# Attention of the first chunks in M2's PSUM banks, v of chunk 1 over ScalarE's queue, M1 begun with one batch, q, k and v prepared one chunk ahead

## Chip, cores, metric

One core of a Trainium2 chip. The metric is the kernel's device time in microseconds (us). The hardware profiler records one execution; its span, from the first to the last instruction, is about 1.8 us shorter than the time of the same run (234.0 against 235.79). Engines: PE is TensorE, DVE VectorE, ACT ScalarE, POOL GpSimd, SP SyncE; ACTq, SPq and POOLq are the profile's lines for ScalarE, SyncE and GpSimd issuing a DMA. The granted clock is the share of full speed that the profile shows for TensorE. A completion semaphore is what a DMA counts up in the built program and a later instruction waits on; the profile puts such a wait down to the DMA's landing (2.17 us for iden in the run before). An eviction is the kernel's copy of a result from a PSUM tile to an SBUF tile (0.59 us on ScalarE and 0.69 on VectorE for 128x512).

## The reference

```python
def _attn_ref(q, k, v):                       # q, k, v: (4 batches, 8 heads, 768, 64)
    gamma = 1.0 - 2.0 ** (-5.0 - np.arange(H, dtype=np.float32))
    for t in range(S):                        # retention: a decayed state per head
        state = gamma[None, :, None, None] * state + np.einsum('bhd,bhe->bhde', k[:, :, t], v[:, :, t])
        y[:, :, t] = scale * np.einsum('bhd,bhde->bhe', q[:, :, t], state)

def _moe_ref(x, w_in, w_out):                 # x: y with heads side by side, (3072, 512); d_ff 2048
    h = x @ w_in
    g = 0.5 * h * (1.0 + np.tanh(c * (h + 0.044715 * h * h * h)))
    return g @ w_out
```

## The kernel before

The 768 positions are worked in 6 chunks of 128. For each chunk and batch, attention is T (transposes of q and k), A (scores, masked on eviction) and Y (y, and the new state S). Then come M1 (h = x w_in by 16 feature blocks of 128 columns, "fc", followed by gelu on ScalarE) and M2 (g w_out). The kernel divides its PSUM banks into tags: att 3, h 3, o 2. Below, v(1,0) means v of chunk 1, batch 0. A unit is one feature block of M1, or a quarter of one batch's M2; a piece is T, A or Y of one batch (T2 is T of batch 2). Units and pieces are dealt in turn, which is meant to keep matmuls running while a piece is evicted. Spin matmuls are fillers without a result.

```python
    def load(c, b):                                   # all of chunk c, batch b over SyncE's queue
        for nm in "qkv":
            load1(nc.sync, nm, c, b)
    def hold(nm, c, b, until):                        # writes one element of a load's buffer:
        nc.gpsimd.tensor_copy(out=ld_tile(nm, c, b)[0:1, 0, 0:1], in_=until)   # the load waits for `until`
    ...
    # --- end of the head ---
    hold("q", 1, 0, w_in_sb[3][0:1, 0, 0:1])
    for b in range(B):
        load(1, b)
    for b in range(B):
        prep(1, b)                                    # q, k scaled, v cast to f16, on GpSimd
        if b == 2:
            for i in range(NO):
                load_w_out(i)                         # GpSimd's queue
    hold("q", 2, 0, w_out_sb[2][0:1, 0, 0:1])
    for b in range(B):
        load(2, b)
    for fc in range(2):
        moe1(0, fc, half, 2 * half)
    for fc in range(2, NF - 1):
        moe1(0, fc)
    ...                                               # attention and M1 of chunk 1
    for b in (0, 2):                                  # M2 of chunk 0: two batches in turn
        for fc in range(NF):
            moe2(0, b, [fc])
            moe2(0, b + 1, [fc])
        ev_O(0, b)
        ev_O(0, b + 1)
    for b in range(B):
        prep(2, b)
    for b in range(B):
        load(3, b)
    zip_units([u for b in range(B) for u in units2(1, b)], pieces(2, STD))
    for c in range(2, NCk):
        if c + 1 < NCk:
            for b in range(B):
                prep(c + 1, b)
        ...
```

## Time and profile before

| | before |
|---|---|
| median of 4 runs | 238.26 us (235.75 to 238.79) |
| profiled run | 235.79 us, span 234.0, granted clock 1.0 |
| TensorE busy | 219.7 us, 94% |
| first M1 at full rate | from 21.95 us |
| M2 of chunk 0 starts | 59.34 us |

Shares of busy time say little here, because the stages have different limits. What a part is worth is read from TensorE's idle stretches, stage by stage. The prediction shows these lines.

### The profile page before, as it was taken

Reading aid. Unit: us, or ns where it says so; the run is one execution under the profiler, and the core shown is the slowest. Engines: PE = TensorE matmul, PEld = TensorE weight load, DVE = VectorE, ACT = ScalarE, POOL = GpSimd, SP = SyncE. Lnnn points to the kernel's source line nnn. Section 1 sums busy time; section 2 is a strip of 40 time slices with the busy share of each in tenths; the row PEclk is TensorE's granted clock in tenths of the full one; section 3 lists DMA queues with packets and bytes.
Section 4 is the critical chain, followed back from the end, with each engine's and each line's share of the span. In section 5 each row is a group of like instructions: output and inputs, shape, how many; then the busy total and the mean of one; then the engine's idle time right before and its main releaser. Section 6 shows DMA issues by size and latency. Waiting matters only on the chain.

```text
span 234.0 us, 3976 instructions
## 1 busy us (share of the span) xinstructions
PE 219.7 (94%) x1623; PEld 117.2 (50%) x1623; DVE 84.2 (36%) x150; ACT 80.3 (34%) x146; POOL 81.1 (35%) x96
## 2 busy tenths in 40 slices
PE   7857998999999999599999999999999999999993
PEld 2435445788534555244544544544554545444453
DVE  3497008760001567424445324444424333200001
ACT  2636661368211111145511155511155511267220
POOL 3584189339650011793101699910000000000000
PEclk9999999999999999999999999999999999999999
DMA  7999999999950988199011199511110011100112
GB/s 177 288 174 181 207 243 199 191 180 237 209 168 39 275 203 249 59 259 254 18 45 45 48 218 233 134 45 45 49 45 0 3 45 45 69 23 0 45 45 90
DMA packets 83537, 29.71 MB, mean 127 GB/s; under 512 B 75584, under 2 KB 80576, under 8 KB 83520
## 3 DMA queue, kind: packets, MB, share of 16 engines
q1 hardware_dynamic: 72528, 23.71, 40.1%
q0 software_dynamic: 4752, 4.19, 12.0%
q10 hardware_dynamic: 6240, 1.57, 3.0%
q8 instruction: 12, 0.20, 0.4%
q14 instruction: 5, 0.04, 0.0%
HBM read 27.37 MB, written 6.29 MB: 144 GB/s over the span
## 4 chain that ended last, share of the span: by engine, by line
PE 83%; DVE 6%; POOL 4%; ACT 3%; issue 2%; DMA 1%; POOLq 0%; DVEq 0%; ACTq 0%
PE h_ps L320 33%; PE o_ps L340 33%; PE qkT_ps L175 4%; PE a_ps L193 3%; PE y_ps L226 3%; PE spin_ps L112 3%; DVE a_sb L206 2%; PE s_ps L238 2%; POOL q L145 2%; POOL k L145 2%; PE y_ps L216 2%; ACT qkT L167 1%; DVE st L257 1%; ACT o_sb L167 1%; DVE xT L169 1%
## 5 line engine op out<-in xcount | busy, mean ns | idle before, releaser
L340 PE MATMUL o_ps<-w_out,g 128*128 128x512 f16 (+1 forms) x400 | 88.8, 371 | 1.0 <-ACT o_sb L167 0.9
L320 PE MATMUL h_ps<-xT,w_in 128*128 128x512 f16 (+1 forms) x456 | 88.6, 346 | 0.2
L329 ACT ACTIVATE g<-h_ps 128x512 f16<-128x512 f32 (+1 forms) x114 | 60.4, 529 | 65.9 <-PE h_ps L320 64.5
L320 PEld LDWEIGHTS <-w_in 128*128 128x128 f16 x456 | 43.0, 98 | 35.3 <-DVE xT L169 0.5
L340 PEld LDWEIGHTS <-g 128*128 128x128 f16 x400 | 37.3, 98 | 39.6 <-issue 1.9
L206 DVE TENSOR_TENSOR a_sb<-a_ps,mask 128x512 f16<-128x512 f32 x48 | 30.9, 686 | 27.3 <-PE a_ps L193 27.3
L167 ACT COPY o_sb<-o_ps 128x512 f32<-128x512 f32 x18 | 10.4, 586 | 70.8 <-PE o_ps L340 66.2
L266 POOL TENSOR_TENSOR stg<-st,cst 128x512 f32<-128x512 f16 x16 | 16.5, 1040 | 49.7 <-DVE st L257 46.4
L169 DVE COPY qkT<-qkT_ps 128x1024 f16<-128x1024 f16 x20 | 13.8, 691 | 35.8 <-PE qkT_ps L175 35.8
L145 POOL TENSOR_TENSOR k<-k,cst 128x512 f16<-128x512 f32 x23 | 24.5, 1063 | 6.2 <-DMA k<-in_k_dram 6.2
L145 POOL TENSOR_TENSOR q<-q,cst 128x512 f16<-128x512 f32 x20 | 20.9, 1044 | 4.9 <-DMA q<-in_q_dram 4.9
L169 DVE CAST xT<-y_ps 128x512 f16<-128x512 f32 x21 | 14.5, 691 | 22.4 <-PE y_ps L226 22.3
L169 DVE COPY o_sb<-o_ps 128x512 f32<-128x512 f32 x5 | 3.5, 692 | 28.7 <-PE o_ps L340 28.7
L257 DVE TENSOR_TENSOR st<-s_ps,stg 64x256 f16<-64x256 f32 x32 | 13.3, 417 | 0.4
L175 PE MATMUL qkT_ps<-iden,q 128*128 128x128 f16 x96 | 9.3, 219 | 3.7 <-DVE a_sb L206 1.9
L142 POOL CAST v<-v 128x512 f16<-128x512 f32 x20 | 12.2, 611 | 1.5 <-DMA v<-in_v_dram 1.4
L193 PE MATMUL a_ps<-qkT 64*128 64x128 f16 x192 | 10.2, 219 | 2.0 <-ACT qkT L167 1.2
L193 PEld LDWEIGHTS <-qkT 64*128 64x128 f16 x192 | 5.6, 94 | 12.1 <-issue 7.6
L112 PE MATMUL spin_ps<-zero 128*128 128x512 f16 x31 | 10.4, 472 | 1.2 <-DVE zero L104 1.2
L175 PEld LDWEIGHTS <-q 128*128 128x128 f16 x96 | 7.1, 98 | 8.7 <-POOL q L145 2.3
L226 PE MATMUL y_ps<-a_sb,v 128*64 128x128 f16 x192 | 10.6, 225 | 0.8 <-DVE a_sb L206 0.7
L175 PE MATMUL qkT_ps<-iden,k 128*128 128x128 f16 x96 | 9.3, 220 | 1.0 <-POOL k L145 1.0
(30 smaller groups left out, 71.8 us busy)
## 6 DMA issues: line engine op xcount, KB each, us to landing
out_dram<-o_sb SPq DMA_DIRECT2D x23, 256.0 KB, 2.0
k<-in_k_dram SPq DMA_DIRECT2D x22, 256.0 KB, 4.2
q<-in_q_dram SPq DMA_DIRECT2D x22, 256.0 KB, 4.0
v<-in_v_dram SPq DMA_DIRECT2D x22, 256.0 KB, 4.4
w_out<-in_moe_w_out_dram POOLq DMA_DIRECT2D x4, 512.0 KB, 10.5
w_in<-in_moe_w_in_dram POOLq DMA_DIRECT2D x3, 512.0 KB, 10.2
q<-in_q_dram ACTq DMA_DIRECT2D x2, 256.0 KB, 3.9
v<-in_v_dram ACTq DMA_DIRECT2D x2, 256.0 KB, 5.0
```

Source lines behind the costliest of these rows:

```text
L112: nc.tensor.matmul(out=ps, lhsT=zero[:, 0:128], rhs=zero, start=True, stop=True)
L145: eng.tensor_tensor(out=t, in0=src, in1=cst[:, col:col + H].unsqueeze(2).broadcast_to([128, H, Dh]), op=ALU.mult,)
L169: eng.tensor_copy(out=out, in_=in_)
L175: nc.tensor.transpose(out=ps[:, i, hp], in_=pair(h16[nm, c, b], hp), identity=iden)
L193: nc.tensor.matmul(out=ps[j][:, hp], lhsT=t[j * 64:(j + 1) * 64, 1, hp], rhs=t[j * 64:(j + 1) * 64, 0, hp], start=True, stop=True,)
L206: nc.vector.tensor_tensor(out=s, in0=ps[j], in1=mask[:, j], op=ALU.mult)
L226: nc.tensor.matmul(out=y_ps[j * 64:(j + 1) * 64, hp], lhsT=vv[:, 2 * hp + j], rhs=a_sb[c, b, j][:, hp], start=(c == 0), stop=True, skip_gr ...
L257: nc.vector.tensor_tensor(out=st[sl, :, b, sl], in0=s_ps[sl, :, sl], in1=stg[sl, :, b, sl], op=ALU.add,)
L266: nc.gpsimd.tensor_tensor(out=stg[:, :, b], in0=st[:, :, b], in1=cst[:, OG:OG + NHP].unsqueeze(2).broadcast_to([128, NHP, 128]), op=ALU.mult,)
L320: nc.tensor.matmul(out=h_ps[:, t0:t1], lhsT=w_in_sb[wi][:, kc, wr * 128:(wr + 1) * 128], rhs=xT[c][:, kc, t0:t1], start=(kc == 0), stop=(k ...
L329: nc.scalar.activation(out=g_sb[c, fc][:, t0:t1], in_=h_ps[:, t0:t1], func=AF.Gelu_apprx_tanh, scale=1.0,)
L340: nc.tensor.matmul(out=ps[:, n0:n1], lhsT=g_sb[c, fc][:, b * C:(b + 1) * C], rhs=w_out_sb[fc // (NF // NO)][:, fc % (NF // NO), n0:n1], st ...
```

## The change

It means to fill TensorE's gaps. In chunks 0 and 1 M2 is not yet running, so its two o banks are free for Y and S, and T and A have the att banks to themselves. M1 of chunk 1 begins as soon as one batch is ready, in units of 128 columns. v of chunk 1 is loaded over ScalarE's queue and cast there, to relieve SyncE and GpSimd. M2 of chunk 0 runs in halves. Chunk c+2 is prepared during the attention of chunk c+1. Outputs of three batches are issued by ScalarE.

```diff
-        y_ps = psum.tile([128, NHP, 128], F32, tag="att", bufs=3, name="y_ps")
+        tag, bufs = ("o", 2) if c < 2 else ("att", 3)
+        y_ps = psum.tile([128, NHP, 128], F32, tag=tag, bufs=bufs, name="y_ps")
 ... (s_ps likewise; spin takes tag "h"; w_in in 4 equal loads; head reordered)
-    hold("q", 1, 0, w_in_sb[3][0:1, 0, 0:1])
+    hold("q", 1, 0, w_in_sb[2][0:1, 0, 0:1])
     for b in range(B):
-        load(1, b)
+        load1(SY, "q", 1, b)
+        load1(SY, "k", 1, b)
     for b in range(B):
-        prep(1, b)
+        prep1(PO, "q", 1, b)
+        prep1(PO, "k", 1, b)
         if b == 2:
             for i in range(NO):
                 load_w_out(i)
     hold("q", 2, 0, w_out_sb[2][0:1, 0, 0:1])
     for b in range(B):
         load(2, b)
+    for fc in range(4, NF):
+        if fc == NF - 1:
+            run1("T0")
+        moe1(0, fc)
+        if fc >= 8 and fc % 2 == 0:
+            load1(AC, "v", 1, (fc - 8) // 2)
+    prep1(AC, "v", 1, 0)
 ... (chunk 1: A0, Y0 T1, M1 of blocks 0 to 9 on batch 0 alone around A1 and Y1, then the rest)
     for b in (0, 2):
-        for fc in range(NF):
-            moe2(0, b, [fc])
-            moe2(0, b + 1, [fc])
-        ev_O(0, b)
-        ev_O(0, b + 1)
+        for f0 in (0, hf):
+            for bb in (b, b + 1):
+                moe2(0, bb, range(f0, f0 + hf))
+                if f0:
+                    ev_O(0, bb)
+        load(3, b)
+        load(3, b + 1)
+        prep(2, b)
+        prep(2, b + 1)
-    zip_units([...units2(1, b)], pieces(2, STD))
+    zip_units([...units2(1, b)], std(2))      # std deals prep of chunk c+1 between the pieces
 ... (ev_O: batches 0 to 2 issue their output from ScalarE's queue)
```

More of the change, by code (lines that the diff above doesn't have):

```diff
@@ L109, in spin @@
     def spin(n):
-        ps = psum.tile([128, 512], F32, tag="o", bufs=2, name="spin_ps")
+        ps = psum.tile([128, 512], F32, tag="h", bufs=3, name="spin_ps")
         for _ in range(n):
@@ L235, in mm_Y @@
         if c + 1 < NCk:
-            s_ps = psum.tile([128, NHP, 128], F32, tag="att", bufs=3, name="s_ps")
+            s_ps = psum.tile([128, NHP, 128], F32, tag=tag, bufs=bufs, name="s_ps")
             for hp in range(NHP):
@@ L285, in att_Y @@
         decay(c, b)
-    w_in_n = (2, 2, 4, 4, 4)
+    w_in_n = (4, 4, 4, 4)
     w_in_at = [sum(w_in_n[:i]) for i in range(len(w_in_n))]
@@ L356, in ev_O @@
         o_sb = op.tile([128, d_model], F32, tag="o", name="o_sb")
-        copy_on(nc.vector if b == B - 1 else nc.scalar, o_sb, ps)
-        nc.sync.dma_start(out=rows, in_=o_sb)
+        if b == B - 1:
+            nc.vector.tensor_copy(out=o_sb, in_=ps)
+            nc.sync.dma_start(out=rows, in_=o_sb)
+        else:
+            nc.scalar.copy(out=o_sb, in_=ps)
+            nc.scalar.dma_start(out=rows, in_=o_sb)
     def moe2_last(c, b):
@@ L374, in moe2_last, with std @@
             nc.sync.dma_start(out=rows[:, m0:m2], in_=o_sb[:, m0:m2])
-    fn = {"T": att_T, "A": att_A, "Y": att_Y}
+    fn = {"T": att_T, "A": att_A, "Y": att_Y, "P": prep}
     def pieces(c, names):
         return [(p[0], c, int(p[1])) for p in names.split()]
-    STD = "T0 T1 A0 T2 A1 Y0 T3 A2 Y1 A3 Y2 Y3"
+    def std(c):
+        todo = pieces(c, "T0 T1 A0 T2 A1 Y0 T3 A2 Y1 A3 Y2 Y3")
+        if c + 1 < NCk:
+            for at, b in ((8, 0), (10, 1), (12, 2), (14, 3)):
+                todo.insert(at, ("P", c + 1, b))
+        return todo
     def zip_units(units, todo, over=None):
@@ L392, in zip_units @@
                 done += 1
-    VE, AC, PO = nc.vector, nc.scalar, nc.gpsimd
+    VE, AC, PO, SY = nc.vector, nc.scalar, nc.gpsimd, nc.sync
     half = 2 * C
@@ L414 @@
     prep1(AC, "v", 0, 1)
+    spin(2)
     mm_Y(0, 0)
     ev_Y(0, 0, AC)
-    spin(2)
     prep1(VE, "q", 0, 2)
     prep1(PO, "k", 0, 2)
-    PO.tensor_copy(out=misc[0:1, 1:2], in_=ld_tile("q", 0, 3)[0:1, 0, 0:1])
-    for i in range(len(w_in_n)):
-        load_w_in(i)
     mm_A(0, 1)
     ev_A(0, 1)
-    ev_S(0, 0)
+    spin(2)
+    PO.tensor_copy(out=misc[0:1, 1:2], in_=ld_tile("q", 0, 3)[0:1, 0, 0:1])
+    load_w_in(0)
+    load_w_in(1)
+    prep1(PO, "k", 0, 3)
+    load_w_in(2)
+    load_w_in(3)
     mm_T(0, 2)
@@ L429 @@
     prep1(AC, "v", 0, 2)
+    prep1(VE, "q", 0, 3)
     mm_Y(0, 1)
     ev_Y(0, 1, AC)
-    spin(2)
-    prep1(VE, "q", 0, 3)
-    prep1(VE, "k", 0, 3)
+    ev_S(0, 0)
+    spin(1)
     mm_A(0, 2)
     ev_A(0, 2)
-    ev_S(0, 1)
+    prep1(AC, "v", 0, 3)
+    spin(3)
     mm_T(0, 3)
-    ev_T(0, 3, AC)
-    spin(2)
+    ev_T(0, 3)
+    mm_Y(0, 2)
+    ev_Y(0, 2, AC)
     mm_A(0, 3)
     ev_A(0, 3)
-    prep1(AC, "v", 0, 3)
-    mm_Y(0, 2)
-    ev_Y(0, 2, AC)
-    ev_S(0, 2)
+    ev_S(0, 1)
+    spin(1)
     moe1(0, 0, 0, half)
+    moe1(0, 1, 0, half)
     mm_Y(0, 3)
     ev_Y(0, 3)
+    ev_S(0, 2)
     ev_S(0, 3)
-    moe1(0, 1, 0, half)
     for b in range(B):
         decay(0, b)
-    hold("q", 1, 0, w_in_sb[3][0:1, 0, 0:1])
+    for fc in range(2, 4):
+        moe1(0, fc, 0, half)
+    for fc in range(4):
+        moe1(0, fc, half, 2 * half)
+    hold("q", 1, 0, w_in_sb[2][0:1, 0, 0:1])
     for b in range(B):
-        load(1, b)
+        load1(SY, "q", 1, b)
+        load1(SY, "k", 1, b)
     for b in range(B):
-        prep(1, b)
+        prep1(PO, "q", 1, b)
+        prep1(PO, "k", 1, b)
         if b == 2:
@@ L466, with run1 @@
         load(2, b)
-    for fc in range(2):
-        moe1(0, fc, half, 2 * half)
-    for fc in range(2, NF - 1):
-        moe1(0, fc)
-    run1 = lambda names: [fn[nm](c, b) for nm, c, b in pieces(1, names)]
-    run1("T0")
-    moe1(0, NF - 1)
-    run1("A0 T1")
-    spin(2)
-    run1("Y0 A1")
-    spin(4)
-    run1("Y1")
-    spin(2)
-    zip_units(
-        [(lambda fc=fc: moe1(1, fc, 0, half)) for fc in range(NF)],
-        pieces(1, "T2 A2 Y2 T3 A3 Y3"),
-    )
+    def run1(names):
+        for nm, c, b in pieces(1, names):
+            fn[nm](c, b)
+    for fc in range(4, NF):
+        if fc == NF - 1:
+            run1("T0")
+        moe1(0, fc)
+        if fc >= 8 and fc % 2 == 0:
+            load1(AC, "v", 1, (fc - 8) // 2)
+    prep1(AC, "v", 1, 0)
+    run1("A0")
+    spin(3)
+    run1("Y0 T1")
+    for fc in range(0, 2):
+        moe1(1, fc, 0, C)
+    prep1(AC, "v", 1, 1)
+    run1("A1")
+    for fc in range(2, 7):
+        moe1(1, fc, 0, C)
+    run1("Y1")
+    for fc in range(7, 10):
+        moe1(1, fc, 0, C)
+    prep1(AC, "v", 1, 2)
+    units = [(lambda fc=fc: moe1(1, fc, C, half)) for fc in range(10)]
+    units += [(lambda fc=fc: moe1(1, fc, 0, half)) for fc in range(10, NF)]
+    units.insert(8, lambda: prep1(AC, "v", 1, 3))
+    zip_units(units, pieces(1, "T2 A2 Y2 T3 A3 Y3"))
     for fc in range(NF):
@@ L492, in units2 @@
         return u
+    hf = NF // 2
     for b in (0, 2):
-        for fc in range(NF):
-            moe2(0, b, [fc])
-            moe2(0, b + 1, [fc])
-        ev_O(0, b)
-        ev_O(0, b + 1)
-    for b in range(B):
+        for f0 in (0, hf):
[5 more added lines that the diff above has]
+        load(3, b + 1)
         prep(2, b)
-    for b in range(B):
-        load(3, b)
-    zip_units([u for b in range(B) for u in units2(1, b)], pieces(2, STD))
+        prep(2, b + 1)
+    zip_units([u for b in range(B) for u in units2(1, b)], std(2))
     for c in range(2, NCk):
-        if c + 1 < NCk:
-            for b in range(B):
-                prep(c + 1, b)
         if c + 2 < NCk:
@@ L515 @@
             units += [u for b in range(B) for u in units2(c, b)]
-            zip_units(units, pieces(c + 1, STD), len(units) - 2)
+            zip_units(units, std(c + 1), len(units) - 2)
         else:
```

## The prediction

> **What bounds the kernel now.** I read the busy shares first, then the chain that ended last, then what TensorE waits for, then the timelines of ScalarE, GpSimd and SyncE's queue.
>
> ```profile
> PE 219.7 (94%) x1623; PEld 117.2 (50%) x1623; DVE 84.2 (36%) x150; ACT 80.3 (34%) x146; POOL 81.1 (35%) x96
> ...
> PE 83%; DVE 6%; POOL 4%; ACT 3%; issue 2%; DMA 1%; POOLq 0%; DVEq 0%; ACTq 0%
> ```
>
> TensorE is busy for 94% of 234.0 us and holds 83% of the chain. A change that leaves the arithmetic alone can win only the rest: TensorE's idle stretches and its fillers. Its list of waits says where they lie:
>
> ```profile
> PE qkT_ps L175 <- DVE a_sb L206: 1.9, 2, 1.2
> PE qkT_ps L175 <- POOL q L145: 1.8, 1, 1.8
> ...
> PE a_ps L193 <- ACT qkT L167: 1.2, 2, 0.7
> PE qkT_ps L175 <- POOL k L145: 1.0, 3, 0.6
> PE o_ps L340 <- ACT o_sb L167: 0.9, 2, 0.5
> ```
>
> (Columns: us in total, times, longest.) The POOL rows are the passage from chunk 2 to chunk 3 (a gap of 2.6 us from 96.6 us in TensorE's timeline; the passage to chunk 4 loses only some 0.4). The o_sb row is the second matmul (M2) of chunk 0; the others are the head, before 21.95 us. Fillers (the spin matmuls) cover part of 35.5 to 41.75 us, where chunk 1's attention starts.
>
> Three more places matter for what the change adds. ScalarE's timeline at the start:
>
> ```profile
> 5.41 0.37 ACTq L77 DMA_DIRECT2D q<-in_q_dram  x1
> 6.09 0.47 ACTq L77 DMA_DIRECT2D v<-in_v_dram  x1
> 6.60 0.62 ACT L140 CAST v<-v 128x512 f16<-128x512 f32 x1 [2.17 <-DMA iden<-rr_ident]
> ```
>
> This cast does not read iden. It waited because the v load ahead of it in ScalarE's stream waited for iden's landing: in the built program the hardware-queue DMAs take eight completion semaphores in turn, in the order in which the kernel's text issues them, and a DMA waits on its issuing engine until the DMA eight places earlier, on whatever queue, has landed. GpSimd's timeline (start, length) and SyncE's queue, with the chain that releases chunk 2's loads:
>
> ```profile
> 25.12 0.18 POOL L88 CAST q<-w_in 1x1 f32<-1x1 f16 x1 [1.34 <-DMA w_in<-in_moe_w_in_dram]
> ...
> 37.61 3.05 POOL L309 DMA_DIRECT2D w_out<-in_moe_w_out_dram  x4
> ...
> 50.63 0.18 POOL L88 CAST q<-w_out 1x1 f32<-1x1 f16 x1 [7.37 <-DMA w_out<-in_moe_w_out_dram]
> ...
> 57.61 1.04 POOL L145 TENSOR_TENSOR q<-q,cst 128x512 f16<-128x512 f32 x1 [0.26 <-DMA q<-in_q_dram]
> ...
> 60.53 1.04 POOL L145 TENSOR_TENSOR q<-q,cst 128x512 f16<-128x512 f32 x1 [0.23 <-DMA q<-in_q_dram]
> ...
> 64.35 0.61 POOL L142 CAST v<-v 128x512 f16<-128x512 f32 x1 [1.22 <-DMA v<-in_v_dram]
> ```
>
> ```profile
> 50.84 0.37 SPq L77 DMA_DIRECT2D q<-in_q_dram  x1
> ...
> 54.45 0.82 SPq L77 DMA_DIRECT2D k<-in_k_dram  x1
> ```
>
> Chunk 2's loads are held until the third w_out block has landed (50.63). The one-element cast at L88 is that hold.
>
> [...] the first 14 fillers take 5.58 us (0.40 each), the next three 0.81 (0.27 each).
>
> **The change, part by part.**
>
> *The v loads of chunk 1 on ScalarE's queue.* They stand in ScalarE's stream after the gelus of feature blocks 8, 10, 12 and 14 of chunk 0, but in the text after all loads of chunk 2. Followed through the built program's semaphores: v(1,0) waits for k(2,1), v(1,1) for q(2,2), v(1,2) for v(2,2), v(1,3) for q(2,3). All four stand behind the hold on w_out. So ScalarE, having done gelu 8 at some 29 us, cannot issue v(1,0) until chunk 2's loads have begun to land, and gelu 9 stands behind it. TensorE has three banks for h and stops at some 31 us. It is no deadlock: GpSimd and SyncE do not need ScalarE to get there.
>
> When does it end? The hold on w_in stays at 25.1 us: the tile waited for again completes the first three quarters of w_in. SyncE then issues 8 loads in place of 12, and GpSimd prepares q and k only. Before, q(1,0) was ready to prepare at 28.7. From there three batches of q and k take 6 x 1.02 = 6.1 us, with loads arriving in step, so w_out is issued at 34.9 in place of 37.61. Issue to hold took 50.63 - 37.61 = 13.0 us; with fewer loads in the way I take 12.2: 47.1 us. k(2,1) was issued 54.45 - 50.84 = 3.6 us after the first load, and loads land about 4.1 us after issue (53.60 to 57.61 for q(2,1)): 47.3 + 3.6 + 4.1 = 55.0 us. By the landings 57.61, 60.53, 64.35 and 65.14 of before, less 3.5 us: q(2,2) 57.0, v(2,2) 60.8, q(2,3) 61.6. ScalarE now does: issue v(1,0), gelus 9 and 10 (0.6 each), issue v(1,1) at 57, gelus 11 and 12 to 59, issue v(1,2) at 60.8 to 61.6, gelus 13 and 14 to 62.8, issue v(1,3) to 63.7, gelu 15 to 64.3, cast of v(1,0) to 64.9. Only then may the y matmuls of chunk 1 start: 65.0, where before they stood at 37.2 to 37.6. This is a shift of some 27.5 us.
>
> *From there to M2 of chunk 0.* Before: 37.6 to 59.4, 21.8 us. After, from the rows by stage: M1 of chunk 1 is 64 x 0.216 = 13.8; batches 2 and 3 of attention 2 x (0.45 + 0.33 + 0.89) = 3.3; the rest of batches 0 and 1 2.3: 19.5 us of TensorE's work. Waits remain: about 1.05 us for qkT of batch 1 (DVE does xT 0.69, the state 0.85, qkT 0.69 first), about 1.3 us because units of 128 columns (0.22 us each) are too short to cover evictions, and ScalarE at an estimated 0.33 us for each narrow gelu. That is 21.85 us, no gain. The clock: TensorE comes out of 24 us of idleness with a few matmuls, so I add 1 us for a slow start. Shift at M2: about +28.5.
>
> *M2 of chunk 0 in halves:* the two waits of 0.46 us go: -0.9.
>
> *Preparing one chunk ahead:* the 2.6 and 0.4 us go. But M2 of chunk 1 is 16 units and chunk 2's attention now 16 pieces with the preparations, so its last y lands after the last unit, where before one unit lay behind it. DVE then copies o (0.69) and evicts y (0.69) before M1 may go on: +0.55. Sum -2.5.
>
> *The head.* With Y and S in the two o banks, each S waits: S1 for the state eviction of batch 0, S2 for y2, Y3 for the eviction of s1, S3 for y3. Walking the durations, feature block 4 starts at about 24.2 us, where before 3.6 blocks were done: -0.3, and it lies before the stall, so it is worth nothing.
>
> *Outputs issued by ScalarE:* 0.33 us each behind a copy of 0.59, in a stage in which ScalarE is idle most of the time; the loads that they must wait for by the rotation land long before. 0.
>
> Sum: 234.0 + 28.5 - 0.9 - 2.5 = 259.1 us of span. The profiled run took 235.79 for a span of 234.0, and the median 238.42, so 1.8 to 4.4 us go on top: I predict 261.
>
> **Rivals.** (1) The intended one: no stall, and the gaps alone go. Then chunk 1 gains 0.3, the head 0.3, M2 0.9, the passages 2.5: 4 us or 1.7%, about 234. What speaks for it: the text issues the v loads early and on another queue, and this would be right if waits were by queue. What speaks against it is the rotation in the program and the 2.17 us wait for iden. (2) The stall is there, but shorter or longer: w_out is DMA-bound (the DMA row reads 9 there), and with fewer competing loads it could land at 45, or k(2,1) in 3 us: 257 or less. Or the later v waits add up with a slow clock through all of chunk 1 (M1 at half speed for 4 us): 265. (3) ScalarE becomes the bound in the narrow-gelu stage: 20 gelus of 0.33 are 6.6 us against 4.4 us of matmuls, but 3.3 us of attention lie between: 1 us more.
>
> **Range and chances.** The chain of holds is certain by the program; its length is a sum of five durations with some 3 us of doubt, the clock 2 and the state of the run 2. Range 253 to 268. Faster only if I misread the rotation: 0.03; within 2%: 0.03; slower: 0.94.
>
> **What would show it.** ScalarE idle between about 29 and 55 us, its wait put down to a k or q load; TensorE empty from about 31 to 55 in the 40 slices (four or five slices near zero); the hold on w_out at about 47; first y matmul of chunk 1 at about 65; no wait for POOL q at the later passages, but some 0.5 us for DVE xT at M1 of chunk 2; no wait for o_sb in M2 of chunk 0. I am wrong if ScalarE's gelus run on through 30 to 36 us, or if chunk 2's k load lands before the w_out hold.

## The result

| | before | after |
|---|---|---|
| median of 4 runs | 238.26 us | 256.77 us (256.46 to 259.85) |
| profiled span | 234.0 | 254.7 |
| mean granted clock | 1.0 | 0.953 |
| TensorE busy | 219.7 us (94%) | 219.9 us (86%) |
| M2 of chunk 0 starts | 59.34 us | 84.56 us |
| from there to the end | 174.7 us | 170.1 us |

The ratio is 1.083, with a 95% interval of 1.072 to 1.094. A ratio is the mean time of one kernel's runs over that of the other's from the same rounds, so it is not quite the ratio of the medians. All these runs count as fast. (The prediction had three of the four runs before, with a median of 238.42.)

The 40 slices of the changed kernel (6.4 us each; tenths of TensorE busy, ScalarE busy, granted clock) show a hole in slices 6 to 8, where before TensorE was full:

```profile
PE   8868900039899999999999999999999999999994
...
ACT  2644400033657310010544112542015621056310
...
PEclk9999965559999999999999999999999999999999
```

The waits of ScalarE and of TensorE in the changed kernel (us in total, times, longest):

```profile
ACT g L331 <- DMA k<-in_k_dram: 24.7, 1, 24.7
...
ACT g L331 <- DMA q<-in_q_dram: 1.0, 1, 1.0
```

```profile
PE h_ps L322 <- ACT g L331: 23.4, 1, 23.4
```

In the kernel a gelu reads its h tile and no k, yet it waited 24.7 us for a load of k. ScalarE's timeline shows what stood ahead of it:

```profile
28.89 0.60 ACT L331 ACTIVATE g<-h_ps 128x512 f16<-128x512 f32 x1 [0.27 <-PE h_ps L322]
53.75 0.38 ACTq L77 DMA_DIRECT2D v<-in_v_dram  x1
54.17 1.08 ACT L331 ACTIVATE g<-h_ps 128x512 f16<-128x512 f32 x2 [24.68 <-DMA k<-in_k_dram]
```

The first v load of chunk 1 could not be issued before 53.75. The next gelu started as soon as it was out. GpSimd's hold of chunk 2 and SyncE's queue give the other end of the chain:

```profile
45.66 0.17 POOL L88 CAST q<-w_out 1x1 f32<-1x1 f16 x1 [6.13 <-DMA w_out<-in_moe_w_out_dram]
```

```profile
45.86 0.37 SPq L77 DMA_DIRECT2D q<-in_q_dram  x1
...
49.22 1.63 SPq L77 DMA_DIRECT2D k<-in_k_dram  x1
```

The k load at 49.22 is k(2,1). With the page's median of 4.3 us from issue to landing it lands at 53.5, just before v(1,0) goes out at 53.75. In the built program v(1,0) waits for two things: the completion semaphore that k(2,1) used last, and the cast of v(0,0), which frees its buffer and is among ScalarE's first instructions. So it is not a buffer that it waits for.

The tail, by TensorE's timelines, stage by stage (us):

| stage | before | after | difference |
|---|---|---|---|
| M2 of chunk 0 | 59.34 to 75.53: 16.19 | 84.56 to 99.24: 14.68 | -1.5 |
| M2 of chunk 1, attention of chunk 2 | to 95.59: 20.06 | to 119.95: 20.71 | +0.65 |
| M1 and M2 of chunk 2 | to 133.48: 37.89 | to 154.70: 34.75 | -3.1 |
| M1 and M2 of chunk 3 | to 168.78: 35.30 | to 189.44: 34.74 | -0.6 |
| the rest | to 234.0: 65.22 | to 254.7: 65.26 | 0 |

The first row in TensorE's timelines, before and after:

```profile
59.34 7.07 PE L340 MATMUL o_ps<-w_out,g 128*128 128x512 f16 x32
66.87 7.34 PE L340 MATMUL o_ps<-w_out,g 128*128 128x512 f16 x32 [0.46 <-ACT o_sb L167]
74.67 1.02 PE L340 MATMUL o_ps<-w_out,g 128*128 128x512 f16 x4 [0.46 <-ACT o_sb L167]
```

```profile
84.56 14.84 PE L342 MATMUL o_ps<-w_out,g 128*128 128x512 f16 x68
```

So the tail won 4.5 us, and the stretch ahead of M2 lost 25.2.

### The profile page after: what moved, and what is told of

It reads as the page before. It is cut to its first block, busy times and chain, and to the rows that moved or that the text cites. A ratio compares the mean times of both kernels' runs of the same rounds, so it can differ in the third digit from the quotient of the medians.

```text
span 254.7 us, 4074 instructions
## 1 busy us (share of the span) xinstructions
PE 219.9 (86%) x1669; PEld 118.9 (47%) x1669; DVE 83.5 (33%) x150; ACT 82.4 (32%) x161; POOL 79.1 (31%) x92
## 4 chain that ended last, share of the span: by engine, by line
PE 71%; DVE 3%; DMA 1%; ACT 1%; issue 0%; DVEq 0%
PE o_ps L342 32%; PE h_ps L322 27%; PE qkT_ps L175 3%; PE y_ps L228 3%; PE a_ps L193 3%; PE s_ps L240 2%; PE y_ps L218 1%; DVE qkT L169 1%; DVE st L259 1%; DMA out_dram<-o_sb 1%; DVE a_sb L206 1%; DVE xT L169 0%; DVE o_sb L360 0%; ACT g L331 0%; ACT v L140 0%
## 5 line engine op out<-in xcount | busy, mean ns | idle before, releaser
L322 PE MATMUL h_ps<-xT,w_in 128*128 128x512 f16 (+2 forms) x504 | 91.2, 332 | 24.6 <-ACT g L331 23.4
L331 ACT ACTIVATE g<-h_ps 128x512 f16<-128x512 f32 (+2 forms) x126 | 61.5, 495 | 89.7 <-PE h_ps L322 60.3
L342 PE MATMUL o_ps<-w_out,g 128*128 128x512 f16 (+1 forms) x400 | 87.8, 371 | 0.0
L322 PEld LDWEIGHTS <-w_in 128*128 128x128 f16 x504 | 44.9, 98 | 58.9 <-issue 26.1
L342 PEld LDWEIGHTS <-g 128*128 128x128 f16 x400 | 37.6, 98 | 39.0
L169 DVE COPY qkT<-qkT_ps 128x1024 f16<-128x1024 f16 x21 | 14.5, 692 | 50.5 <-PE qkT_ps L175 50.2
L145 POOL TENSOR_TENSOR k<-k,cst 128x512 f16<-128x512 f32 x24 | 25.1, 1044 | 7.4 <-DMA k<-in_k_dram 7.4
L193 PE MATMUL a_ps<-qkT 64*128 64x128 f16 x192 | 9.5, 219 | 2.1 <-DVE qkT L169 1.6
L240 PE MATMUL s_ps<-v,k 128*128 128x128 f16 x80 | 7.9, 221 | 2.5 <-DVE st L257 1.0
L142 POOL CAST v<-v 128x512 f16<-128x512 f32 x16 | 9.7, 609 | 0.2 <-DMA v<-in_v_dram 0.2
```

What stands on the lines that cost most here:

```text
L145: eng.tensor_tensor(out=t, in0=src, in1=cst[:, col:col + H].unsqueeze(2).broadcast_to([128, H, Dh]), op=ALU.mult,)
L169: eng.tensor_copy(out=out, in_=in_)
L193: nc.tensor.matmul(out=ps[j][:, hp], lhsT=t[j * 64:(j + 1) * 64, 1, hp], rhs=t[j * 64:(j + 1) * 64, 0, hp], start=True, stop=True,)
L240: nc.tensor.matmul(out=s_ps[:, hp], lhsT=pair(kk, hp), rhs=pair(vv, hp), start=True, stop=True)
L322: nc.tensor.matmul(out=h_ps[:, t0:t1], lhsT=w_in_sb[wi][:, kc, wr * 128:(wr + 1) * 128], rhs=xT[c][:, kc, t0:t1], start=(kc == 0), stop=(k ...
L331: nc.scalar.activation(out=g_sb[c, fc][:, t0:t1], in_=h_ps[:, t0:t1], func=AF.Gelu_apprx_tanh, scale=1.0,)
```

## The experiments

Theory: the built program's eight completion semaphores tie v of chunk 1 to loads of chunk 2 that are held back, and ScalarE stands still behind the v load (24.7 us in the trace above). Rival A: loads issued on ScalarE's queue are slow, or the v transfers lose bandwidth to the weights. Rival B: the new head, the o banks and the narrow M1 units cost the time.

### The v loads ahead in the text

```diff
-    hold("q", 2, 0, w_out_sb[2][0:1, 0, 0:1])
-    for b in range(B):
-        load(2, b)
     ...
     for fc in range(4, NF):
         ...
             load1(AC, "v", 1, (fc - 8) // 2)
+    hold("q", 2, 0, w_out_sb[2][0:1, 0, 0:1])
+    for b in range(B):
+        load(2, b)
```

> The hold and the loads of chunk 2 are moved in the text behind the v loads of chunk 1. Every engine keeps the same instructions in the same order; only the completion semaphores change hands (v(1,0) to v(1,3) now wait for q and k of chunk 0 and of batch 1 of chunk 1, all landed by some 32 us). My theory: ScalarE's wait of 24.7 us goes, y of chunk 1 starts at 37.2 us, M2 of chunk 0 at 59.8 (22.6 us later as measured), the end 170.1 us after that: span 229.9, time 231.7 (229 to 234). Rival A, that loads issued on ScalarE's queue are slow or that the v transfers lose bandwidth to the weights: about 256.8 still, since queue, bytes and order are unchanged.

Measured: 231.77 us (median of 5, 231.54 to 233.75), ratio to before 0.977 (0.971 to 0.983). Each engine's instructions and their order were compared and are the same; the semaphores of the loads and the buffers that the v tiles rotate through differ (the buffers are no rival: see the two waits of v(1,0) above). The 24.7 us are gone. These are ScalarE's longest waits now, none of them on a load of chunk 2:

```profile
ACT o_sb L363 <- PE o_ps L342: 67.3, 18, 5.9
ACT g L331 <- PE h_ps L322: 65.7, 89, 6.6
ACT o_sb L379 <- DMA out_dram<-o_sb: 3.2, 1, 3.2
```

The profiled run is the slowest of the five (233.75): its first M1 waited 1.6 us for w_in, and the clock was at 0.56 to 0.59 from 22 to 26 us; the other four ran at 0.997 to 1.0. So y of chunk 1 starts at 38.86 and M2 of chunk 0 at 61.87 in this trace, where 37.2 and 59.8 were expected; from M2 to the end it takes 170.1 us, as expected. Each v load now goes out while the gelus run on:

```profile
31.11 0.60 ACT L331 ACTIVATE g<-h_ps 128x512 f16<-128x512 f32 x1 [0.27 <-PE h_ps L322]
31.12 0.37 ACTq L77 DMA_DIRECT2D v<-in_v_dram  x1
31.98 0.60 ACT L331 ACTIVATE g<-h_ps 128x512 f16<-128x512 f32 x1 [0.27 <-PE h_ps L322]
```

Rival A is out: queue, bytes and engine order stayed, and 25 us went. So is rival B: head, o banks and narrow units are all still there.

### v of chunk 1 on SyncE's queue

```diff
         load1(SY, "k", 1, b)
+        load1(SY, "v", 1, b)
     ...
-        if fc >= 8 and fc % 2 == 0:
-            load1(AC, "v", 1, (fc - 8) // 2)
```

> The v loads of chunk 1 go back to SyncE's queue, between q and k of their batch; ScalarE still casts them. My theory: no wait of ScalarE on a load of chunk 2; time as of the kernel with the moved text, 231 to 234. Rival A expects the same here, so this run tells only with the other. Rival B, that the narrow gelus, the o banks and the new order of the head cost the 18 us: still about 256.

Measured: 231.85 us (one run). It confirms the first experiment by another way, and shows at clock 0.998 what the intended parts are worth. M2 of chunk 0 starts at 59.97, where before it started at 59.34: the new head and chunk 1 win nothing. TensorE's waits say why:

```profile
PE a_ps L193 <- DVE qkT L169: 1.6, 3, 0.9
...
PE s_ps L240 <- DVE st L257: 1.0, 1, 1.0
PE y_ps L228 <- DVE st L257: 0.9, 1, 0.9
PE s_ps L240 <- DVE xT L169: 0.8, 1, 0.8
PE s_ps L240 <- ACT xT L167: 0.7, 1, 0.7
```

With two banks for Y and S, four matmul groups of the head wait for the eviction of an earlier Y or S: 3.4 us in the last four rows. The first row is chunk 1: 0.9 us for qkT of batch 1, which DVE evicts behind xT and the state, and 0.3 and 0.4 us where units of 128 columns (two in 0.61 us, three in 1.05 us by TensorE's timeline) ended before DVE's eviction of qkT (0.69 us once begun). The old waits were replaced by new ones of about the same size: leaving out the first filler's 1.2 us, TensorE's listed waits ahead of M2 sum to 5.3 us before and 6.3 here, with three fillers in chunk 1 in place of eight.

### Chunk 2 held for the first w_out block instead of the third

```diff
-    hold("q", 2, 0, w_out_sb[2][0:1, 0, 0:1])
+    hold("q", 2, 0, w_out_sb[0][0:1, 0, 0:1])
```

> The changed kernel with chunk 2's hold on the first w_out block instead of the third. My theory: the hold ends when that block lands, at 34.4 + 5.6 = 40.0 us in place of 45.7; k(2,1) follows 8.0 us later, perhaps 1 us more because w_out still comes in: 48 to 49 in place of 53.7; the whole kernel ends some 5 us earlier: 251.5 (250 to 254). Rival A: no earlier, or later, since loads and weights now compete: 257 to 260.

Measured: 257.03 us (one run), so the expectation missed, and the number lies where rival A's forecast had it (257 to 260). The hold did end at 40.0 us. But SyncE's queue in this run reads:

```profile
40.22 0.37 SPq L77 DMA_DIRECT2D q<-in_q_dram  x1
...
41.26 5.35 SPq L77 DMA_DIRECT2D v<-in_v_dram  x1
46.71 3.45 SPq L77 DMA_DIRECT2D q<-in_q_dram  x1
50.20 0.85 SPq L77 DMA_DIRECT2D k<-in_k_dram  x1
```

v(2,0) took 5.35 us to issue (1.35 in the changed kernel) and q(2,1) 3.45 (0.83), while the rest of w_out came in; its slowest block took 13.2 us to land instead of 11.4. k(2,1) went out at 50.20, and ScalarE issued v(1,0) at 54.36. The tie holds, but what set the length of the stall here was the transfers ahead of k(2,1), not the hold: the hold ended 5.6 us earlier (40.02 against 45.66), and k(2,1) went out 1.0 us later (50.20 against 49.22). So loads and weights were both slower in this run, in which they overlapped longer, as rival A said; but it was ahead of k(2,1) and not at the v loads, which took 0.37 to 0.42 us each to issue. This run is no evidence on how the stall's length scales with the hold; it only fails to contradict the theory.

### Only batch 0 of chunk 2 ahead of the v loads

```diff
     hold("q", 2, 0, w_out_sb[2][0:1, 0, 0:1])
-    for b in range(B):
-        load(2, b)
+    load(2, 0)
     ...
             load1(AC, "v", 1, (fc - 8) // 2)
+    for b in range(1, B):
+        load(2, b)
```

> Only batch 0 of chunk 2 stays ahead of the v loads in the text. By the built program v(1,0), v(1,1) and v(1,2) then wait for k of chunk 1 (landed by 31, 33.4 and 35 us), but v(1,3) still for q(2,0), which stands behind the hold. My theory: ScalarE stops after gelu 14 at some 36 us until q(2,0) lands at about 45.9 + 4 = 50 us; then gelu 15, the cast and y of chunk 1 at about 51.2 instead of 61.9; with a slow clock at first 1 to 2 us lost: span 245.5, time 247 (245 to 250). Rival A: as the changed kernel, 256. If only the first of the four waits counted: 232.

Measured: 248.8 us (one run, span 247.0). ScalarE stopped where the semaphores said, at the fourth v load and not at the first:

```profile
36.54 0.38 ACTq L77 DMA_DIRECT2D v<-in_v_dram  x1
36.97 1.09 ACT L331 ACTIVATE g<-h_ps 128x512 f16<-128x512 f32 x2 [2.36 <-PE a_ps L193]
51.84 0.40 ACTq L77 DMA_DIRECT2D v<-in_v_dram  x1
52.29 0.60 ACT L331 ACTIVATE g<-h_ps 128x512 f16<-128x512 f32 x1 [14.23 <-DMA q<-in_q_dram]
```

The hold ended 2 us later than assumed (47.9), and w_out's slowest block took 14.3 us to land instead of 11.4; three v loads went out from 31.25 to 36.92, but that they are the cause is not shown. q(2,0) was issued at 48.12, and v(1,3) went out at 51.84. With one tied load of four ScalarE still stood for 14.2 us, and the run is 17.0 us longer than the median with the moved text, because that release (51.84) comes almost as late as that of v(1,0) in the changed kernel (53.75).

### The v loads on ScalarE's queue alone, in the kernel before

```diff
-        load(1, b)
+        load1(nc.sync, "q", 1, b)
+        load1(nc.sync, "k", 1, b)
     for b in range(B):
-        prep(1, b)
+        prep1(PO, "q", 1, b)
+        prep1(PO, "k", 1, b)
     ...
     for fc in range(2, NF - 1):
         moe1(0, fc)
+        if fc >= 8 and fc % 2 == 0:
+            load1(AC, "v", 1, (fc - 8) // 2)
     ...
+    prep1(AC, "v", 1, 0)
 ... (casts of the other three: one before Y0 A1, two after Y1)
```

> The kernel before with this one part alone: v of chunk 1 on ScalarE's queue, at the same places after gelus 8, 10, 12 and 14, and cast by ScalarE; head, o banks, M1 units, M2 and preparation as before. By the built program the four loads wait for k(2,0), v(2,0), q(2,1) and k(2,1). My theory: ScalarE idle from about 29.7 to 50.4 us, y of chunk 1 at about 58 instead of 37.5: span 255, time 256.5 (253 to 259), so that this part alone makes more than the whole loss. If the loss needed the other parts as well: under 245.

Measured: 260.96 us (one run), 23.4 above the median before, above the range that was expected (253 to 259). I had named the tied loads wrongly: read again, the built program ties v(1,0) to v(1,3) to k(2,1), v(2,1), q(2,2) and k(2,2), one batch later than written. k(2,1) was issued at 49.98, and ScalarE moved on 4.0 us later:

```profile
54.02 0.41 ACTq L77 DMA_DIRECT2D v<-in_v_dram  x1
54.47 1.08 ACT L329 ACTIVATE g<-h_ps 128x512 f16<-128x512 f32 x2 [23.89 <-DMA k<-in_k_dram]
```

Y of chunk 1 begins at 62.2 instead of 37.05, and the span is 25.1 us longer: the shift is the whole loss. So this one part makes all of it without the others.

### The tail alone, and one unit more behind the last y

The head and chunk 1 of before are joined with the changed kernel from M2 of chunk 0 on. The second and third kernels also deal chunk 2's pieces over 15 units of M2 instead of 16:

```diff
-    zip_units([u for b in range(B) for u in units2(1, b)], std(2))
+    zip_units([u for b in range(B) for u in units2(1, b)], std(2), 4 * B - 1)
```

> The kernel before up to the end of M1 of chunk 1, the changed kernel from M2 of chunk 0 on (M2 in halves, preparation one chunk ahead, outputs issued by ScalarE). From the traces the changed tail is 174.5 - 170.1 = 4.4 us shorter, and the changed head and chunk 1 win nothing at full clock (59.5 to M2 before, 59.97 with v on SyncE). So 4.4 us faster than before run for run: ratio 0.981. If the new head holds the clock better (the kernel before ran at 0.978 to 1.0, the one with moved text at 0.989 to 1.0), this kernel keeps the spread of the one before and ends about 1 us behind the kernel with v on SyncE.

> The same, and chunk 2's pieces are dealt over 15 units instead of 16, so that one unit of M2 lies behind the last y. The wait of 0.48 us for xT at the first M1 of chunk 2 goes: 0.5 us faster than without, ratio to before 0.979.

> The changed kernel with v of chunk 1 on SyncE's queue and with 15 units: 231.85 - 0.5 = 231.3 us, ratio to before 0.975; if its head holds the clock better than before's, 1 us ahead of the one with before's head, otherwise equal to it within 0.3 us.

| kernel | median of 6 runs | ratio to before (95%) | granted clock |
|---|---|---|---|
| tail only | 232.62 us (231.53 to 234.17) | 0.981 (0.975 to 0.986) | 0.985 to 0.993 |
| tail, 15 units | 231.55 us (230.57 to 233.29) | 0.977 (0.971 to 0.983) | 0.971 to 0.997 |
| all of the change with v on SyncE, 15 units | 231.25 us (231.08 to 232.53) | 0.975 (0.971 to 0.980) | 0.991 to 1.0 |

The tail brings all of the gain, as the traces said (0.981). Against a bound of 2% only the last kernel is clearly faster; the intervals of the other two, and of the kernel with the moved text, reach above 0.98. The wait of 0.5 us for xT, there in the tail-only trace, is missing in both traces with 15 units; as a difference in time (0.981 to 0.977) it lies inside the intervals. The last kernel beats both kernels of this study clearly. Whether its head holds the clock better is not settled: its runs are closer together and at a higher clock, but its ratio is within 0.2% of that of the kernel with the old head.

## Why the prediction was right

**The mechanism.** It said that ScalarE stops behind a v load whose semaphore belongs to a held load of chunk 2. The wait of 24.7 us, the run with the moved text (no such wait, 231.77 us) and the run with one tied load (14.2 us) show it.

**One statement in it was too simple:** that semaphores are dealt in the order of the kernel's text. They are dealt in the order of the built program, which is not the text's. With the moved text, v(1,0) stands there between k(1,1) and q(1,2), although its text comes after all of chunk 1's q and k. In the changed kernel itself q(3,0) stands between v(1,0) and v(1,1), although its text comes much later. A variant that I built and did not run kept q(2,0) and k(2,0), but no v, ahead in the text; its v loads of chunk 1 stood early too. So it seems to be the v tiles of chunk 2, which share a rotation of buffers with those of chunk 1, that pushed them back. This is argued from builds, not shown.

**The length of the stall.** Predicted: hold 47.1, k(2,1) landed 55.0, first y of chunk 1 at 65.0. Measured: 45.66, 53.75 (issue of v(1,0)), 61.93. Of the 3.1 us, 1.4 lie in the hold: w_in's hold ended at 24.3 instead of 25.1, so w_out was issued at 34.44 instead of 34.9 (the prediction's own terms sum to 34.8), and it needed 11.2 us from issue instead of 12.2. From the hold to the release it took 0.2 us more than reckoned. The other 1.8 lie behind the release: the third v load left at 59.17, not 60.8, the last at 60.09, not 62.8, and gelus 14 and 15 ran without a wait between them. Rival (2) of the prediction, w_out landing at 45 and a time of 257 or less, came nearer than its main figure of 261.

**From the first y to M2.** Predicted 21.85 us and 1 for a slow clock, which was the author's estimate; measured 22.63. That the sum of 22.85 is so near is partly luck: the clock cost nothing here, and the rest took 0.8 us more than reckoned. In the kernel before this stretch is 22.3 us, since its first y matmul that reads v starts at 37.05 in the trace and not at 37.2 to 37.6, as the prediction read. The clock's 1 us was wrong in kind. The granted clock did fall to 0.50, and was back at 1.00 before the first y of chunk 1 at 61.93 (stretch, length, busy us of PE, PEld, DVE, ACT and POOL, granted clock, DMA share, GB/s):

```profile
35.00:54.00 19.00, 0.00 (x0) 0.00 (x0) 0.00 (x0) 0.00 (x0) 4.71 (x7) 0.50 1.07 192
...
56.00:58.00 2.00, 2.00 (x7) 0.78 (x6) 0.00 (x0) 1.09 (x2) 0.00 (x0) 0.59 1.23 277
58.00:60.00 2.00, 2.00 (x17) 1.05 (x15) 0.50 (x1) 0.39 (x1) 0.00 (x0) 1.00 1.28 290
```

The slow matmuls (12 in 4.13 us from 54.82, where 12 take 2.75 at full clock) are the rest of M1 of chunk 0, which had to wait for ScalarE anyway. The narrow gelu, put at 0.33 us by an estimate whose source the prediction does not name, takes 0.25 (1.25 for five), so ScalarE was no bound.

**M2 of chunk 0:** predicted -0.9, measured -1.5. I took the two idle times of 0.46 us as the cost; but idle time is counted from a matmul's modelled end: the trace lists a 128x512 matmul at 0.379 us, and in an unbroken row they start 0.216 us apart (64 in 13.81 us), so the end lies 0.16 us behind the point at which the next could have started. So they cost 0.62 and 0.61 us, and a third wait of 0.27, between the first two matmuls after 66.87 (ScalarE's copy of the second bank ran to 67.30), is not listed at all.

**The passages:** predicted -2.6, -0.4 and +0.55; measured -3.1, -0.6 and +0.65. The 2.6 us are in the trace three idle times, of 1.81, 0.60 and 0.21, and three times 0.16 is the missing 0.5; that the other two differ for the same reason is likely, not shown. The wait for xT at M1 of chunk 2 is 0.48 us.

**Outputs issued by ScalarE:** predicted 0, and nothing in the tail contradicts it.

Sum: predicted span 259.1, measured 254.7. Of the difference of 4.4, 3.1 is the stall, 0.2 the stretch to M2, and 1.1 the tail; all three errors had the same sign, and the range of 253 to 268 held them.

## What to carry to other kernels

Before moving a load to another engine's queue, look in the built program at which earlier DMA its completion semaphore waits for. Here that one was held back on SyncE's queue, and ScalarE stood still with all that was behind its v load: 24.7 us in the changed kernel, 23.9 with the v loads alone moved, 14.2 with one tied load. In the order of the built program, no load that a compute engine is to issue early should stand behind a load with a hold. Of a large change with several parts, compare start times of the same stage in both traces: here a tail of -4.5 us was hidden under a loss of 25.

## Semaphores, issue times and the clock, as measured

- In the built program the completion semaphores are dealt in rotation over the loads of several queues, so that a load on one engine waits for one on another: 24.7 us here, between v(1,0) on ScalarE's queue and k(2,1) on SyncE's.
- SyncE took 0.37 to 2.4 us to issue one 256 KB load of q, k or v in the changed kernel, with a median of 4.3 to 4.6 us from issue to landing, and up to 5.35 us to issue one with the early hold, while w_out came in.
- In the changed kernel the granted clock fell to 0.50 at 33.75 us, 2.3 us after the last matmul (31.45), and was back at 1.00 at 57.64, 2.8 us after matmuls resumed (54.82). With one tied load matmuls resumed at 53.44, where eight of y took 0.64 us; the eight of y at 58.92 took 0.41. In the run with the moved text the granted clock was 1.00 from 20 to 22 us, 0.56 from 22 to 24 and 0.59 from 24 to 26; TensorE's longest listed wait before that was 1.6 us, for w_in, to 19.91. At the start the first 14 fillers took 5.58 us (0.40 each), the next three 0.81 (0.27 each). The profile prints a granted clock of 1.00 there, but the trace's clock record begins only at 6.05 us (6.45 in the changed kernel), so their clock is not shown.
